# Moving the weight conversion's intermediate word to PSUM, and the products with v beside the scores

## The chip, the cores and the metric

The kernel runs on one core of a Trainium2 chip. The core has a matrix engine (TensorE, PE), a vector engine (VectorE, DVE), a scalar engine (ScalarE, ACT), GpSimd (POOL), and SyncE (SP), whose queue here issues most of the DMAs. Each engine takes its instructions in order and they wait for one another through semaphores. PSUM, into which PE writes, has eight banks of 512 fp32 words for each of 128 partitions. The metric is the device time of the whole program in microseconds, as the median of several executions.

## What is computed

Attention of 4 sequences, 8 heads, 576 positions and 64 dimensions, half the heads with a band of 32 and half with a stride of 32 as mask; then a dense layer pair (512 to 2048 to 512) on the 2304 tokens, and a mixture of 8 experts with two chosen per token. Cut to what matters:

```python
def reference(q, k, v, w_in, w_out, w_gate, w_noise, noise, w1, w2):
    scores = q @ k.transpose(0, 1, 3, 2) / 8              # masked: band of 32, or stride of 32
    attn = softmax(where(mask, scores, -1e9))
    x = merge_heads(attn @ v)                             # 2304 x 512
    h = x @ w_in                                          # 512 -> 2048
    x = (h * sigmoid(1.702 * h)) @ w_out                  # 2048 -> 512
    top2, weight = route(x @ w_gate + softplus(x @ w_noise) * noise)
    for e in range(8):
        for k in range(2):
            m = top2[:, k] == e
            out[m] += weight[m, k] * (relu(x[m] @ w1[e]) @ w2[e])
    return out
```

## The kernel before

The tokens lie in six chunks of 384. The first dense layer pair has 16 pieces `fc` of 128 hidden units; for each chunk and piece `m1_l1` makes the hidden units (12 matmuls of 128x384: three for each of four parts of the model dimension, since every operand is split into a high and a low part) and `m1_l2` adds their share to the output (9 matmuls of 128x512) one iteration later. The order is written out by hand for PE, ACT, DVE and POOL in this part. Chunk 0 is done in two halves (`SEGS`): pieces 0 to 7 (`HALFC` is 8), which I call the first half chunk, then chunk 1, then the rest of chunk 0.

Attention is worked in groups. For one group `scores` makes q·k on PE (L208 or L223), DVE masks them out of PSUM and finds the row's extreme (L171), ACT takes exponents (L176), DVE sums up and inverts (L180, L182), POOL normalizes the early groups (L184), PE transposes the weights (L236 or L241), ACT copies them (L237 or L242), PE multiplies with v (`values`, `g_av`, L254 or L264), and `put_x` splits these products into a high part (ACT, L192) and a low part (DVE, L195). A loop ahead of the first chunk works the first groups; the next ones are threaded into the first half chunk, two in each iteration: behind `m1_l1` PE does products, transposes and scores of three different groups, and behind `m1_l2` the same again.

Weights of the first layer pair arrive as 64-bit words and are converted. A piece is 128x512; `w_bits` does three DVE operations on it: L387 makes an intermediate word `cv` from the high halves, L390 works on it in place, L394 joins it with the low halves into the raw tile `area`. Then ACT casts the result (L361) and POOL forms the low part (L362). The operations of one piece are spread over an iteration (`conv`, one `next` at a time), one piece in odd iterations and two in even ones of the first half chunk; six pieces are converted in the loop ahead of it.

PSUM in the first half chunk: banks 0 and 1 hold the first layer's sums (`ps`), 2 to 4 the second layer's, 5 the scores, 6 the transposes, 7 the products. The loop ahead of it uses 0 to 2 for scores, 3 and 4 for transposes, 5 and 6 for products. `cv` lies in SBUF, in one buffer.

Of the kernel before, what the change touches and what calls it, by code (L numbers as in the profile page):

```python
# [12 lines left out]
I32 = mybir.dt.int32  # L13
# [20 lines left out]
GQ = RPG * NI  # L34
NG = -(-BAND // RPG)
KW = 96
# [63 lines left out]
def tile_kernel(ctx, tc, qkL, qkS, vL, vS, wm1, wm2, wgn, noise, cst, lst0, out):  # L100
# [5 lines left out]
    PB = [psum.tile([128, 512], F32, tag=f"pb{i}", name=f"pb{i}") for i in range(8)]  # L106
# [13 lines left out]
    with ExitStack() as main, tc.manual_schedule(engines={mybir.EngineType.PE}):  # L120
# [4 lines left out]
        tmp = main.enter_context(tc.tile_pool(name="tmp", bufs=2))  # L125
# [8 lines left out]
        def xtile(c):  # L134
            X[c] = xtp.tile([128, 2, 4, CH], F32R, tag="xt", name=f"xt{c}")
# [54 lines left out]
        def put_x(parts, conv):  # L190
            for hi, lo, src in parts:
                nc.scalar.copy(hi, src)  # L192
            next(conv, None)
            for hi, lo, src in parts:
                nc.vector.tensor_sub(lo, src, hi.bitcast(F32))  # L195
# [46 lines left out]
            nc.scalar.copy(pt[:n, :2 * n], PB[bank][:n, :2 * n])  # L242
            return pt

        def g_av(gr, ld, pt, bank, conv):
            b, pr, g = gr
            v = ld[1]
            if pr < 2:
                pb = PB[bank][:, :3 * KW].rearrange("p (t w) -> p t w", w=KW)
                for t in range(3):  # L250
                    for h in range(2):
                        o = 128 * t + 64 * h
                        w = 64
                        nc.tensor.matmul(pb[64 * h:64 * h + 64, t, :w], v[:KW, t, 64 * h:64 * h + 64],  # L254
                                         pt[:KW, o:o + 64], start=True, stop=True)
                c, o = divmod(b * S + 192 * g, CH)
                hi, lo = (X[c][:, i, pr, o:o + 192].rearrange("p (t q) -> p t q", q=64) for i in range(2))
                put_x([(hi, lo, pb[:, :, :64])], conv)
                return
            n = min(GQ, S - GQ * g)  # L260
            nr = n // NI
            pb = PB[bank]
            for h in range(2):
                nc.tensor.matmul(pb[64 * h:64 * h + 64, :n], v[:n, 0, 64 * h:64 * h + 64],  # L264
                                 pt[:n, n * h:n * h + n], start=True, stop=True)
            src = pb[:, :n].rearrange("p (r i) -> p r i", i=NI)
            i0 = 0
            parts = []
            while i0 < NI:
                c, o = divmod(b * S + BAND * i0, CH)  # L270
                ni = min(NI - i0, (CH - o) // BAND)
                hi, lo = (X[c][:, i, pr, o:o + BAND * ni].rearrange("p (i r) -> p r i", r=BAND)
                          [:, RPG * g:RPG * g + nr, :] for i in range(2))
                parts.append((hi, lo, src[:, :, i0:i0 + ni]))
                i0 += ni
            put_x(parts, conv)

        class Attention:
# [34 lines left out]
                    self.pt[i] = g_trans(self.gs[i], self.ld[i], self.sm.pop(i)[0], banks[i % len(banks)])  # L313
                    self.nc += 1

            def values(self, banks, conv=iter(())):
                while self.done < self.nc:
                    i = self.done
                    g_av(self.gs[i], self.ld[i], self.pt.pop(i), banks[i % len(banks)], conv)
                    self.done += 1  # L320


# [48 lines left out]
        def w_step():  # L371
            left = 512
            while PIECES and left:
                fc, s, raw, o, n = PIECES[0]
                if n < 512:
                    if len(done) < born[0] + LATE:
                        return
                    born.pop(0)
                PIECES.pop(0)
                left -= n  # L380
                yield from w_bits(fc, s, raw, o, n)

        def w_bits(fc, s, raw, o, n):
            t = tmp.tile([128, n], I32, tag="cv", name="cv", bufs=1)
            low, high = raw[:, :, 0], raw[:, :, 1]
            w32 = raw.rearrange("p n t -> p (n t)")[:, :n]
            nc.vector.tensor_scalar(t, high, 3, 0x3FFFFFFF,  # L387
                                    op0=OP.logical_shift_left, op1=OP.bitwise_and)
            yield
            nc.vector.scalar_tensor_tensor(t, high, -0x40000000, t,  # L390
                                           op0=OP.bitwise_and, op1=OP.bitwise_or)
            yield

            nc.vector.scalar_tensor_tensor(w32, low, 29, t,  # L394
                                           op0=OP.logical_shift_right, op1=OP.bitwise_or)
            SPLIT[-1].append((fc, s, w32.bitcast(F32), o, n))
            yield
# [10 lines left out]
        def m1_part():  # L408
            for j in range(TPC):
                p = stp.tile([128, DM], F32, tag="raw", name="part")  # L410
                if j == 1:
                    nc.vector.tensor_scalar(p, PB[2 + j], 0.5, None, op0=OP.mult)
                else:
                    nc.scalar.mul(p, PB[2 + j], 0.5)
                PART.append(p)
# [21 lines left out]
        def m1_split(c, t, g):  # L437
            nc.scalar.copy(g[:, 0], t)  # L438
            eng = nc.vector if c or fc >= HALFC else nc.gpsimd
            eng.tensor_sub(g[:, 1], t, g[:, 0].bitcast(F32))  # L440
# [283 lines left out]
        att = Attention(sum(parts, []), upto[1], upto[1])  # L724
# [9 lines left out]
        while att.done < upto[0] - REM:  # L734
            conv = w_step() if k in CONVAT else iter(())
# [37 lines left out]
        def drain():  # L773
            while fill:
                step()

        def finish(c, bank=[7]):
            while att.done < upto[c]:
                att.values([7])
                att.norms()  # L780
                att.transposes([6])

        seq = [(c, fc) for c, a, b in SEGS for fc in range(a, b)]
        for i, (c, fc) in enumerate(seq):
            if i and (c, fc) in FIRST:
                drain()
            if fc == 0:
                for k in {2: (3, 4), 3: (5,)}.get(c, ()):
                    xtile(k)
                if 0 < c < len(parts):  # L790
                    finish(c)
                if c + 1 < len(parts):
                    att.limit = upto[c + 1]
            conv = w_step()
            t, g = m1_l1(c, fc, step, conv)
            att.values([7])
            att.transposes([6])
            next(conv, None)
            att.scores([5])
            next(conv, None)  # L800
            m1_split(c, t, g)
            att.exps()
            for _ in conv:
                pass
            w_split()
            conv = w_step() if i < HALFC and not i % 2 or i >= SMALLS else iter(())
            att.norms(conv)
            if c == 3 and fc in (4, 6, 8, 10, 12):
                clear(x2d, 64 * fc - 256, 1)
            if c == 1 and fc == 12:  # L810
                chained(lst.rearrange("(p n) t -> p (n t)", p=128),
                        lst0.rearrange("(p n) t -> p (n t)", p=128), True)
            if c == 4 and fc % 2:
                clear(out, CH * (fc // 2), min(TPC, NT + NBLK - TPC * (fc // 2)))
            if c == NCHUNK - 1 and fc == 6:
                drain()
                e_list(0, 0, NA // 128, nc.gpsimd)
                fill.append(e_part(0, 0, N + DUMP - CH, wait=WAIT0))
            if c == NCHUNK - 1 and fc == 10:
                e_list(1, 0, NA // 128, nc.gpsimd)  # L820
                pre1 = e_part(1, 0, N + DUMP - CH)
                next(pre1)
            if c == NCHUNK - 1 and fc >= 8:
                w2_load(fc - 8)
            if i:
                m1_l2(*seq[i - 1], step)
                if i == HALFC:
                    m1_part()
                elif seq[i - 1] in LAST:
                    fill.insert(0, routing(seq[i - 1][0], [6], 7))  # L830
            att.values([7], conv)
            next(conv, None)
            att.transposes([6])
            if i < HALFC:
                att.scores([5])
            att.load(2)
            for _ in conv:
                pass
            w_split()
            if i < HALFC:  # L840
                att.exps()
                att.norms()
            if (c, fc) == (NCHUNK - 2, NFC - 1):
                fine.close()
# [38 lines left out]
        for h in range(H0, H1):  # L883
            e, fc = divmod(h, NF2)
# [44 lines left out]
    with tc.tile_pool(name="ovf", bufs=1) as op:  # L929
        n = nc.values_load(nrow[:, 0:1], min_val=0, max_val=NJ)  # L930
        with tc.For_i(0, n, 1) as j:
# [10 lines left out]
            pb = PB[7].rearrange("p (k t) -> p k t", t=128)  # L942
# [3 lines left out]
            w = op.tile([128, NF2, 1024], F32, name="ow")  # L946
# [80 lines left out]
```

## Time and profile before

| | us |
|---|---|
| median of 3 runs | 1027.28 (1025.06 to 1028.02) |
| profiled execution | 1031.41 |
| its span, first to last instruction | 1029.6 |
| PE busy | 994.2 (97%) |
| DVE busy | 489.3 (48%) |
| ACT busy | 394.6 (38%) |
| POOL busy | 219.4 (21%) |

The profile is of one execution, and its span is what the rows below add up to. A busy share over the whole span is a mean over stages with different limits: PE's 97% comes from the long part with the dense layers and the experts, while at the start other engines are the busier ones. The stages that matter here are the loop ahead of the first chunk (to 40.9 us), the first half chunk with early attention in it (to about 94 us, the last of that attention's scores at 81 us), and the rest.

### The profile page before, as it was taken

To read this page: it belongs to the slowest core of one execution; us is meant where nothing else is said; L and a number is where in the kernel's file an instruction comes from. 1 tells how busy PE (TensorE), PEld (TensorE's weight loads), DVE (VectorE), ACT (ScalarE), POOL (GpSimd) and SP (SyncE) were. 2 spreads that over 40 slices of the span, in tenths; PEclk is the share of its full clock that TensorE was granted. 3 is DMA by queue.
4 is the path that set the end of the run, shared out by engine and by line. 5 is a ranking of instruction groups with operands and counts; after the bars stand their busy time and mean duration, and the time that the engine had idled before them with its cause. 6 is when DMAs were issued, how large, how long until landed. Compare 5 with 4: busy or idle time off the path is not lost. (4 is left out here: it accounts for less than half of the span.)

```text
span 1029.6 us, 16148 instructions
## 1 busy us (share of the span) xinstructions
PE 994.2 (97%) x5804; PEld 881.0 (86%) x5804; DVE 489.3 (48%) x1520; ACT 394.6 (38%) x1075; POOL 219.4 (21%) x206
## 2 busy tenths in 40 slices
PE   6999999999999999999999999999999999999996
PEld 5778898988888888899978888989999899998995
DVE  6979864447446544523645353342434343333310
ACT  5665533244444444323433242232424233332311
POOL 3465221102000200200410413040322205041302
PEclk9699999999999999999999999999999999999999
DMA  8835512022131325301342154263544527163403
GB/s 293 281 120 189 175 62 72 1 79 51 47 101 49 70 83 197 109 1 63 78 147 73 32 164 114 81 137 110 122 125 89 157 70 177 62 145 119 84 2 52
DMA packets 63393, 107.69 MB, mean 105 GB/s; under 512 B 12096, under 2 KB 25536, under 8 KB 63296
## 3 DMA queue, kind: packets, MB, share of 16 engines
q1 hardware_dynamic: 53104, 85.63, 26.1%
q0 software_dynamic: 10208, 21.02, 10.7%
q8 instruction: 46, 0.75, 0.3%
q14 instruction: 35, 0.29, 0.1%
HBM read 84.04 MB, written 22.73 MB: 104 GB/s over the span
## 5 line engine op out<-in xcount | busy, mean ns | idle before, releaser
L672 DVE SCALAR_TENSOR_TENSOR ht<-pb,ht 128x384 fp32r<-128x384 f32 (+1 forms) x128 | 62.5, 488 | 251.7 <-ACT ht L671 250.7
L671 ACT ACTIVATE ht<-pb 128x384 fp32r<-128x384 f32 (+1 forms) x128 | 56.0, 437 | 259.4 <-PE pb L670 251.0
L426 PE MATMUL pb<-xt,w 128*128 128x384 f32 x384 | 134.5, 350 | 0.0
L428 PE MATMUL pb<-xt,w 128*128 128x384 f32 x384 | 129.3, 337 | 0.0
L427 PE MATMUL pb<-xt,w 128*128 128x384 f32 x384 | 129.2, 336 | 0.1
L702 POOL DMA_INDIRECT out<-y,ix x40 | 64.9, 1623 | 295.0 <-ACT y L701 262.1
L685 PE MATMUL pb<-w,ht 128*128 128x512 f32 x320 | 127.7, 399 | 0.0
L686 PE MATMUL pb<-w,ht 128*128 128x512 f32 x320 | 125.3, 392 | 0.0
L687 PE MATMUL pb<-w,ht 128*128 128x512 f32 x320 | 125.1, 391 | 0.0
L450 PE MATMUL pb<-w,g 128*128 128x512 f32 x288 | 118.8, 412 | 3.5 <-ACT g L438 2.5
L451 PE MATMUL pb<-w,g 128*128 128x512 f32 x288 | 114.0, 396 | 0.8 <-POOL w L362 0.8
L433 DVE SCALAR_TENSOR_TENSOR th<-th,pb 128x384 f32<-128x384 f32 x96 | 52.9, 551 | 129.9 <-ACT th L431 124.0
L452 PE MATMUL pb<-w,g 128*128 128x512 f32 x288 | 114.6, 398 | 0.0
L575 POOL DMA_INDIRECT lst<-pay,si x36 | 36.3, 1007 | 348.0 <-DVE si L572 292.4
L593 DVE TENSOR_TENSOR w<-raw,w 128x512 fp32r<-128x512 f32 x128 | 84.0, 689 | 18.6 <-ACT w L592 15.3
L431 ACT ACTIVATE th<-pb 128x384 f32<-128x384 f32 x96 | 46.9, 489 | 109.8 <-PE pb L428 101.3
L668 PE MATMUL pb<-xa,w 128*128 128x384 f32 x256 | 87.2, 340 | 0.0
L670 PE MATMUL pb<-xa,w 128*128 128x384 f32 x256 | 86.3, 337 | 0.0
L669 PE MATMUL pb<-xa,w 128*128 128x384 f32 x256 | 85.9, 336 | 0.0
L592 ACT CAST w<-raw 128x512 fp32r<-128x512 f32 x128 | 74.0, 618 | 18.6 <-DMA raw<-wm 14.5
L438 ACT CAST g<-th 128x384 fp32r<-128x384 f32 x96 | 49.3, 513 | 76.7 <-DVE th L433 75.3
L427 PEld LDWEIGHTS pb<-xt,w 128*128 128x128 f32 x384 | 72.5, 189 | 2.6 <-DVE st L180 0.4
(175 smaller groups left out, 1970.9 us busy)
## 6 DMA issues: line engine op xcount, KB each, us to landing
raw<-wm SPq DMA_DIRECT2D x136, 256.0 KB
area<-wm SPq DMA_DIRECT2D x28, 512.0 KB
out<-zero SPq DMA_DIRECT2D x7, 768.0 KB
qk<-qkL SPq DMA_DIRECT2D x16, 304.0 KB
att<-qkS SPq DMA_DIRECT2D x20, 189.0 KB
qk<-qkS SPq DMA_DIRECT2D x20, 189.0 KB
v<-vL SPq DMA_DIRECT2D x16, 192.0 KB
att<-qkL SPq DMA_DIRECT2D x8, 304.0 KB
```

What stands on the lines that cost most here:

```text
L426: nc.tensor.matmul(ps, w[0][:, a], X[c][:, 0, kc, :], start=(kc == 0), stop=False)
L427: nc.tensor.matmul(ps, w[0][:, a], X[c][:, 1, kc, :], start=False, stop=False)
L428: nc.tensor.matmul(ps, w[1][:, a], X[c][:, 0, kc, :], start=False, stop=(kc == 3))
L450: nc.tensor.matmul(o, g[:, 0, a], w[0], start=((c, fc) in FIRST), stop=False)
L451: nc.tensor.matmul(o, g[:, 0, a], w[1], start=False, stop=False)
L452: m = nc.tensor.matmul(o, g[:, 1, a], w[0], start=False, stop=((c, fc) in LAST))
L668: nc.tensor.matmul(ps, w[:, 0, a], x[:, 0, kc, :], start=(kc == 0), stop=False)
L669: nc.tensor.matmul(ps, w[:, 0, a], x[:, 1, kc, :], start=False, stop=False)
L670: nc.tensor.matmul(ps, w[:, 1, a], x[:, 0, kc, :], start=False, stop=(kc == 3))
L685: nc.tensor.matmul(o, g[:, 0, a], w[:, 0, 512:], start=(fc == 0), stop=False)
L686: nc.tensor.matmul(o, g[:, 0, a], w[:, 1, 512:], start=False, stop=False)
L687: m = nc.tensor.matmul(o, g[:, 1, a], w[:, 0, 512:], start=False, stop=(fc == NF2 - 1))
```

## The change

`w_bits` gets its intermediate word from its caller. While the list `INPS` is not empty it is a part of PSUM bank 7, seen as 32-bit integers, and no longer the SBUF tile `cv`; `INPS` is emptied in iteration 8, when the first half chunk's sums have been put away. Since bank 7 then holds that word, the products of `values` go to bank 5, to columns 288 and up, behind the scores, which take columns 0 to 287. In `g_av` the three blocks of a banded group stand 64 columns apart and no longer 96, so that they fit. `finish`, which does single groups at the end of a part, and the loop ahead of the first chunk keep their banks.

```diff
-        def g_av(gr, ld, pt, bank, conv):
+        def g_av(gr, ld, pt, bank, conv, off):
...
-                pb = PB[bank][:, :3 * KW].rearrange("p (t w) -> p t w", w=KW)
+                pb = PB[bank][:, off:off + 192].rearrange("p (t w) -> p t w", w=64)
...
-                put_x([(hi, lo, pb[:, :, :64])], conv)
+                put_x([(hi, lo, pb)], conv)
...
-            pb = PB[bank]
+            pb = PB[bank][:, off:off + GQ]
...
-            def values(self, banks, conv=iter(())):
+            def values(self, banks, conv=iter(()), off=0):
...
-                    g_av(self.gs[i], self.ld[i], self.pt.pop(i), banks[i % len(banks)], conv)
+                    g_av(self.gs[i], self.ld[i], self.pt.pop(i), banks[i % len(banks)], conv, off)
...
+                yield from w_bits(fc, s, raw, o, n, PB[7][:, 512 - left:][:, :n].bitcast(I32) if INPS else None)
                 left -= n
-                yield from w_bits(fc, s, raw, o, n)
-
-        def w_bits(fc, s, raw, o, n):
-            t = tmp.tile([128, n], I32, tag="cv", name="cv", bufs=1)
+
+        INPS = [True]
+
+        def w_bits(fc, s, raw, o, n, t):
+            if t is None:
+                t = tmp.tile([128, n], I32, tag="cv", name="cv", bufs=1)
...
-            att.values([7])
+            vb = [5] if INPS else [7]
+            vo = 3 * KW if INPS else 0
+            att.values(vb, off=vo)
...
                     m1_part()
+                    INPS.clear()
...
-            att.values([7], conv)
+            att.values(vb, conv, vo)
```

No instruction changes its place on any engine. What the instructions write and wait for does. On PE, in iteration 0 behind the first layer, before (`pb_68` is bank 5, `pb_69` bank 6, `pb_70` bank 7; L254 products, L236 transposes, L208 scores; in brackets the semaphores, named by the engine or DMA queue that raises them):

```order
L254 MATMUL pb_70<-att 64x64 [waits DMAHW3_49,DVE_49,Activation_49]
L254 MATMUL pb_70<-att 64x64 x5
L236 MATMUL pb_69<-cs,att 96x128 [waits Pool_49]
L236 MATMUL pb_69<-cs,att 96x128 x2
L208 MATMUL pb_68<-att 128x96 [waits DMAHW1_49]
L208 MATMUL pb_68<-att 128x96 x2
L254 MATMUL pb_70<-att 64x64 [waits DMAHW5_49,DVE_49,Activation_49]
```

On PE at the same place, now:

```order
L254 MATMUL pb_68<-att 64x64 [waits DMAHW3_49,Activation_49]
L254 MATMUL pb_68<-att 64x64 x5
L236 MATMUL pb_69<-cs,att 96x128 [waits Pool_49]
L236 MATMUL pb_69<-cs,att 96x128 x2
L208 MATMUL pb_68<-att 128x96 [waits DMAHW1_49,DVE_49]
L208 MATMUL pb_68<-att 128x96 x2
L254 MATMUL pb_68<-att 64x64 [waits DMAHW5_49,DVE_49,Activation_49]
```

The products have moved to the scores' bank, and the wait for DVE has moved from the products to the scores behind them. In the built program the count that these scores wait for is the one that DVE reaches with L195 of the products two rows above. From the second pair on both have a wait for DVE, before and now; there the scores' count was that of the last masks (L171) and is now that of L195 of the products just made, and the products' count was that of the last L195 and is now that of the last masks.

On DVE, in iteration 0, where two pieces are converted, from the end of the first piece to the reading of the second products, before (`area` is a raw tile, `st` the statistics of a group, `xt` the split products):

```order
L394 SCALAR_TENSOR_TENSOR area<-area,cv 128x512 [waits DVE_49]
L387 TENSOR_SCALAR cv<-area 128x512 [waits DMAHW0_49,DVE_49]
L180 TENSOR_SCALAR st<-st 128x3 [waits Activation_49]
L390 SCALAR_TENSOR_TENSOR cv<-area,cv 128x512 [waits DVE_49]
L182 RECIPROCAL st<-st 128x3 [waits DVE_49]
L394 SCALAR_TENSOR_TENSOR area<-area,cv 128x512 [waits DVE_49]
L195 TENSOR_TENSOR xt_107<-pb_70,xt_107 128x192 [waits Activation_49]
```

On DVE at the same place, now:

```order
L397 SCALAR_TENSOR_TENSOR area<-area,pb_70 128x512 [waits DVE_49]
L390 TENSOR_SCALAR pb_70<-area 128x512 [waits DMAHW0_49,DVE_49]
L180 TENSOR_SCALAR st<-st 128x3 [waits Activation_49]
L393 SCALAR_TENSOR_TENSOR pb_70<-area,pb_70 128x512 [waits DVE_49]
L182 RECIPROCAL st<-st 128x3 [waits DVE_49]
L397 SCALAR_TENSOR_TENSOR area<-area,pb_70 128x512 [waits DVE_49]
L195 TENSOR_TENSOR xt_107<-pb_68,xt_107 128x192 [waits Activation_49]
```

The word is in bank 7 and the order is the same: L195, for which the next scores now wait, stands behind the operations on two pieces. (Lines behind L379 have moved by three or more: L387, L390 and L394 are L390, L393 and L397 in the changed kernel. This text uses the numbers of before.)

## Rows read from the trace of the kernel before

**Rows 1.** Stages: length; busy PE, PEld, DVE, ACT, POOL; PEclk, DMA share, GB/s.

```profile
25.00:40.90 15.90, 13.98 (x73) 10.70 (x73) 15.55 (x71) 11.18 (x52) 7.76 (x11) 0.50 0.98 343
40.90:80.90 40.00, 36.91 (x260) 29.56 (x259) 32.03 (x123) 25.20 (x99) 24.06 (x26) 0.99 0.48 153
80.90:94.00 13.10, 12.80 (x74) 10.34 (x73) 12.05 (x30) 7.07 (x26) 8.63 (x8) 1.00 0.43 152
94.00:1029.60 935.60, 914.07 (x5278) 816.46 (x5276) 414.31 (x1225) 336.11 (x839) 171.61 (x150) 1.00 0.34 93
```

**Rows 2.** Timeline, iteration 4: start us, length us, engine, line, operation, tiles.

```profile
73.30 0.35 PE L264 MATMUL pb<-att 72*64 72x72 f32 x4
...
74.35 0.48 PE L450 MATMUL pb<-w,g 128*128 128x512 f32 x1
...
76.58 0.44 PE L264 MATMUL pb<-att 126*64 126x126 f32 x4
...
77.22 0.60 PE L223 MATMUL pb<-att 128*126 128x126 f32 x4
...
79.77 0.43 DVE L195 TENSOR_TENSOR xt<-pb,xt 128x42 fp32r<-128x42 f32 x2
```

**Rows 3.** DVE's groups by line and shape, 0 to 40.9 us.

```profile
L390 DVE SCALAR_TENSOR_TENSOR cv<-area,cv 128x512 int32<-128x512 int32 x6 | 7.5, 1250 | 0.0
L394 DVE SCALAR_TENSOR_TENSOR area<-area,cv 128x512 int32<-128x512 int32 x6 | 5.1, 850 | 0.2
L387 DVE TENSOR_SCALAR cv<-area 128x512 int32<-128x512 int32 x6 | 4.3, 715 | 0.0
```

**Rows 4.** Timeline of DVE and POOL: a conversion operation beside GpSimd, and undisturbed ones.

```profile
17.97 1.35 POOL L362 TENSOR_TENSOR w<-area,w 128x512 fp32r<-128x512 f32 x1 [1.08 <-ACT w L361]
...
18.22 1.64 DVE L394 SCALAR_TENSOR_TENSOR area<-area,cv 128x512 int32<-128x512 int32 x1
...
48.48 0.43 DVE L387 TENSOR_SCALAR cv<-area 128x512 int32<-128x512 int32 x1
...
48.94 0.69 DVE L390 SCALAR_TENSOR_TENSOR cv<-area,cv 128x512 int32<-128x512 int32 x1
```

**Rows 5.** DVE operations with PSUM as input: L433 to 100 us, L412 whole span.

```profile
L433 DVE SCALAR_TENSOR_TENSOR th<-th,pb x9: 541/547/555, 45.5 to 97.5; 128x384 f32<-128x384 f32 x9
...
L412 DVE TENSOR_SCALAR part<-pb x1: 687/687/687, 101.8 to 101.8; 128x512 f32<-128x512 f32 x1
```

**Rows 6.** Timeline: the first and the last of the eleven scores, and their L195.

```profile
45.74 0.81 PE L208 MATMUL pb<-att 128*128 128x96 f32 x6
...
45.97 0.35 DVE L195 TENSOR_TENSOR xt<-pb,xt 128x192 fp32r<-128x192 f32 x1
...
80.93 0.42 PE L223 MATMUL pb<-att 128*72 128x72 f32 x4
...
82.48 0.45 DVE L195 TENSOR_TENSOR xt<-pb,xt 128x42 fp32r<-128x42 f32 x2
```

**Rows 7.** Timeline: scores B of iterations 0 to 3, and pair A of iteration 1.

```profile
47.51 0.70 PE L223 MATMUL pb<-att 128*126 128x126 f32 x4
...
50.73 0.57 PE L254 MATMUL pb<-att 96*64 96x64 f32 x12 [0.43 <-issue]
...
51.46 0.62 ACT L361 CAST w<-area 128x512 fp32r<-128x512 f32 x1 [2.51 <-PE pb L254]
...
54.38 0.35 DVE L195 TENSOR_TENSOR xt<-pb,xt 128x192 fp32r<-128x192 f32 x1
...
55.80 0.70 PE L223 MATMUL pb<-att 128*126 128x126 f32 x4
...
63.53 0.48 PE L223 MATMUL pb<-att 128*72 128x72 f32 x4 [0.16 <-DVE st L171]
...
70.60 0.65 PE L223 MATMUL pb<-att 128*126 128x126 f32 x4
```

**Rows 8.** Timeline of PE: the idle time ahead of the half clock.

```profile
25.41 0.69 PE L264 MATMUL pb<-att 126*64 126x126 f32 x4 [1.62 <-DVE xt L195]
```

## Prediction

> **What bounds the kernel now.** I read the busy time of each engine by stage first, then the instructions of single iterations in order of time. The table by stage [rows 1] says that from 94.0 us on TensorE (PE) works 914.07 of 935.60 us at a granted clock of 1.00, that is 2.4 GHz: its queue is full there, and whatever is lost earlier the end inherits. From 25.0 to 40.9 us VectorE (DVE) is busy 15.55 of 15.90 us, while PE, at a clock of 0.50 (1.2 GHz), is busy 13.98: this is the attention in front of the first chunk, and DVE bounds it. From 40.9 to 80.9 us the first half chunk runs, with the rest of the early attention threaded between its matmuls: PE is busy 36.91 of 40.00 and has 3.1 us of slack, no more.
>
> An iteration of that half chunk holds two pairs of products with v and scores: pair A behind the first layer, pair B behind the second; I number them by the iteration, from 0. In iteration 4 PE has no gap [rows 2]: products A at 73.30, scores A just ahead of the second layer at 74.35, products B at 76.58, scores B at 77.22. Scores B of iteration 3 began at 70.60 [rows 7], so a dense iteration takes 6.6 us: 2.7 from scores B to products A, 1.05 to the second layer, 2.2 to products B, 0.65 to scores B.
>
> **What the change removes.** The word of 128x512 that the first conversion operation (L387) writes and the other two (L390, L394) read leaves SBUF, where the raw word lies too. Six pieces are converted in the first 40.9 us, L390 at 1250 ns in the mean, L394 at 850, L387 at 715 [rows 3]. Undisturbed they take 0.69 and (L387) 0.43 us [rows 4]; the rest is time beside GpSimd, as when L394 starts at 18.22 us while L362 runs there (from 17.97, for 1.35 us) and takes 1.64. L433, with one input in PSUM and one in SBUF, is never stretched: 541 to 555 ns in nine runs [rows 5]. The two long operations become of that kind.
>
> What will they cost? No row has DVE writing PSUM. Nearest are a tensor_scalar of 128x512 that reads PSUM, 687 ns [rows 5], and the undisturbed L390, 0.69 us. Below that I see no gain, since no row of such a shape with two inputs or one in PSUM is shorter; above, an operation that reads and writes one bank (L390) might take twice as long, 1.4 us. I take 0.69 for all three and keep 1.4 for the range. Then 18 x 0.69 = 12.4 us stand in place of 7.5 + 5.1 + 4.3 = 16.9 [rows 3]: DVE saves 4.5 us. PE caps it: its 13.98 of 15.90 us at half clock leave 1.9 us behind 25.0, and the two pieces before that save some 2. I take **3 us** gained (1 to 4.5; none if L390 takes 1.4, since 6 x 0.7 = 4.2).
>
> **What it adds.** The products leave bank 7, which the word now fills, for the scores' bank 5. The order of instructions stays the same on every engine; PE's waits change. Scores had to wait for the reading of the scores before them; now they wait until DVE's L195 has read the products that PE made just ahead of them, in the same bank though in other columns. PE takes its queue in order, so behind the waiting scores stands a whole first layer (12 matmuls) or second layer (9), the very work with which PE runs ahead of DVE today. Eleven scores, A0 to A5, come to stand so, and PE starts each before its L195 has ended: A0 at 45.74, with the end at 45.97 + 0.35; A5 at 80.93, with the end at 82.48 + 0.45 [rows 6]. Over the eleven this lead adds up to 25.9 us. That would be the price if each L195 stayed where it is; but DVE is late partly because PE ran ahead. So I go round the loop by hand, from the start of scores B (zero), with the durations of these rows.
>
> - *Pair A, plain.* Products at 2.7; tanh 0.5, L433 0.55, L195 0.45 and about 0.2 for hand-overs: scores A at 4.4 in place of 3.4. The second layer follows, products B come at 7.0.
> - *Pair B, odd iteration* (one piece converted). Masks, L394 and the short operations are done by 7.0, ScalarE copies the products, L195 ends at 7.9: scores B at 8.0.
> - *Pair B, even iteration.* A second piece lies ahead of L195 on DVE: masks to 5.6, then L394, L387, L390 and L394 at 0.69 and two short ones at 0.17, L195: scores B at 9.2. In the trace this L195 ends at 79.77 + 0.43, 3.0 us behind the start of scores B at 77.22 [rows 2].
> - *Iterations 1 and 2.* ScalarE's L361 stands ahead of exponents and tanh and waits for products A (idle 2.51 us until L254 [rows 7]); from products A at 50.73 to the end of L195 at 54.38 + 0.35 it is 4.0 us. With 0.26 more for L387, scores A come 2.55 later than in the plain case: 10.5 us for iteration 1, 11.75 for 2.
> - *Iteration 0* has no second layer: products B must also wait for the masks of scores A, and two pieces stand ahead of their L195. Scores B move from 47.51 to 51.35.
>
> Against the trace's scores B at 47.51, 55.80, 63.53, 70.60 and 77.22 and scores A5 at 80.93 [rows 7, 2, 6]: +3.85 for iteration 0, 10.5 - 8.3 = +2.2 for 1, 11.75 - 7.7 = +4.0 for 2, 8.0 - 7.1 = +0.9 for 3, 9.2 - 6.6 = +2.6 for 4, 4.4 - 3.7 = +0.7 for the first part of 5: **+14.2 us**. From below: a plain A costs 1.0 over the dense iteration, an odd B 0.4, an even B 1.6, so 6 x 1.0 + 2 x 0.4 + 3 x 1.6 = 11.6, less the slack of 3.1: 8.5. From above: L390 at 1.4 lies twice on the way of an even B and once of an odd one, 3 x 1.4 + 2 x 0.7 = 5.6 more: 19.8.
>
> Nothing hides it: PE is busy 12.80 of 13.10 us up to 94.0 and nearly always after [rows 1]. Later pieces keep the old form, and the DMAs keep their order, so I cost both at nothing.
>
> In the built program the scores wait although the columns are disjoint. The Trainium skill speaks against this placing too: PSUM — Partial Sum Buffer, section Summary: rules for kernel authors, has PSUM read in another bank than the one a matmul writes, guarded by bank. By that rule the sum stays +14.2; with a guard by columns it would be 0 and the kernel would gain the 3 us.
>
> **The rivals.** (1) *DVE's time wins.* If scores did not really stand (the waits met early, or guarded by columns), the front's 3 us would be left: 1024.3. For it: DVE bounds the stage up to 40.9 us. Against it: tanh, L433 and L195 alone end 1.7 us behind the products, and the eleven waits would have to cost under 1.4 us in all even with the full 4.5 gained. (2) *PE absorbs it.* At the lower bound of the waits and the upper of the gain, less hand-overs that overlap better than I lay them, +5 - 4.5: 1028, which a measurement of this kernel can't tell from no change (0.3%, 3.1 us). (3) *The clock falls too.* PE stood 1.62 us for an L195 up to 25.41 us [rows 8], and the stage from 25.0 on has a clock of 0.50 [rows 1]. I expect three stalls of more than 2 us (B0, A1, A2). If each brings the half clock for the 2.2 us of layer behind it, 3 x 2.2 = 6.6 us more: 1045. Against it: between the stalls PE is denser here than it was there. By the Trainium skill (TensorE: Matmul & The Clock Gate, Part 1: The HAM clock gate) activity releases the throttle and its absence brings it back; long enough stalls would make 1045 the rule.
>
> **How the numbers follow.** -3.0 + 14.2 = +11.2 us. The profiled execution took 1031.41 us (span 1029.6), 4.1 above the median of the runs; I put the difference on the median: 1027.28 + 11.2 = **1038.5 us**. Chances: forecast (+3.1 to +20) 0.66, clock 0.18, absorbed 0.10, DVE's time 0.06. So faster by over 0.3% 0.06, within 0.3% 0.10, slower 0.84. For 8 in 10 I leave out the faster case, most of the absorbed one and the clock rival's upper part: 1029.5 to 1047, the latter being the upper bound, +19.8 without the front's gain.
>
> **What would show it.** Right: the three operations on the word near 0.69 us and none stretched; PE idle ahead of the eleven scores, 1 to 3.6 us each, until L195; the first layer starting about 3 us before 40.89 us, the way from there to scores A5 14 us longer, and what follows as long as before. Wrong: no idle time ahead of these scores; operations of 1.2 us or more on the word, which would eat the gain in front; a clock of 0.50 between 45 and 80 us, which would add rival 3 to the sum.

## The result, and the profile after

The changed kernel takes 1041.28 us (median of four runs, 1040.17 to 1042.15), the kernel before 1026.90 beside it (1025.06 to 1028.02): 14.4 us more, a ratio of 1.0142 with a 95% interval of 1.0124 to 1.0159. The profiled execution took 1040.70 us (span 1038.9), close to its median, while that of before was 4.1 us above its own; so the two traces differ by 9.3 us, and stretches are compared rather than ends. From L387 on, the line numbers of the changed kernel are 3 higher: the word's operations are L390, L393 and L397, the first layer begins at L429 in place of L426, and the second at L453 in place of L450.

The stages of after, cut where the same work begins and ends (first layer 36.88, scores A5 98.30, second chunk 111.1), with the columns of [rows 1]:

```profile
25.00:36.88 11.88, 10.15 (x62) 7.79 (x59) 11.00 (x63) 9.54 (x47) 6.73 (x9) 0.64 1.03 374
36.88:98.30 61.42, 46.39 (x261) 35.85 (x259) 34.05 (x124) 27.35 (x103) 22.78 (x26) 0.82 0.39 126
98.30:111.10 12.80, 12.80 (x72) 10.43 (x73) 9.42 (x25) 6.25 (x21) 6.54 (x7) 1.00 0.32 102
111.10:1038.90 927.80, 911.40 (x5278) 815.84 (x5276) 409.66 (x1224) 335.85 (x838) 171.46 (x150) 1.00 0.35 93
```

The first layer starts 4.0 us earlier than at 40.89 us. From there to scores A5 it takes 61.42 us where before took 40.04 (80.93 - 40.89), at a granted clock of 0.82 in place of 0.99, with PE busy 46.39. That is 4.0 won and 21.4 lost. The second chunk starts at 110.96 us against 93.90: 17.1 late in these two traces. In the medians 14.4 us are left at the end.

DVE's groups on the word in the front (0 to 36.9 us), against [rows 3]:

```profile
L393 DVE SCALAR_TENSOR_TENSOR pb<-area,pb 128x512 int32<-128x512 int32 x6 | 4.1, 688 | 0.0
L390 DVE TENSOR_SCALAR pb<-area 128x512 int32<-128x512 int32 x6 | 4.1, 687 | 0.0
L397 DVE SCALAR_TENSOR_TENSOR area<-area,pb 128x512 int32<-128x512 int32 x6 | 4.1, 687 | 0.2
```

The sum is 12.3 us in place of 16.9. No operation is stretched any more; L393, which reads and writes one bank, is at 688 ns not longer than the others.

PE's timeline: the first layer's start, and the eleven scores with the idle time ahead of each:

```profile
36.88 0.67 PE L429 MATMUL pb<-xt,w 128*128 128x384 f32 x1
...
42.50 0.91 PE L208 MATMUL pb<-att 128*128 128x96 f32 x6 [0.47 <-DVE xt L195]
...
47.26 1.22 PE L223 MATMUL pb<-att 128*126 128x126 f32 x4 [1.97 <-DVE xt L195]
...
56.54 1.21 PE L223 MATMUL pb<-att 128*126 128x126 f32 x4 [3.25 <-DVE xt L195]
...
63.25 0.70 PE L223 MATMUL pb<-att 128*126 128x126 f32 x4 [0.41 <-DVE xt L195]
...
70.23 1.22 PE L223 MATMUL pb<-att 128*126 128x126 f32 x4 [3.43 <-DVE xt L195]
...
76.87 0.48 PE L223 MATMUL pb<-att 128*72 128x72 f32 x4 [0.47 <-DVE xt L195]
...
81.09 0.70 PE L223 MATMUL pb<-att 128*126 128x126 f32 x4 [0.84 <-DVE xt L195]
...
85.20 0.70 PE L223 MATMUL pb<-att 128*126 128x126 f32 x4 [0.71 <-DVE xt L195]
...
89.50 0.70 PE L223 MATMUL pb<-att 128*126 128x126 f32 x4 [0.84 <-DVE xt L195]
...
93.92 0.70 PE L223 MATMUL pb<-att 128*126 128x126 f32 x4 [0.93 <-DVE xt L195]
...
98.30 0.48 PE L223 MATMUL pb<-att 128*72 128x72 f32 x4 [0.84 <-DVE xt L195]
```

Every one stands for L195 (PE sits idle, with these scores next in its queue), as the prediction said; in the trace of before none of the eleven did. Eight stand under 1 us, three (B0, A1, A2) 2 to 3.4. Why A1 stands that long is seen in all engines between its products and its start:

```profile
52.26 0.57 PE L254 MATMUL pb<-att 96*64 96x64 f32 x12
...
52.99 0.62 ACT L361 CAST w<-area 128x512 fp32r<-128x512 f32 x1 [7.18 <-PE pb L254]
...
54.29 0.47 ACT L434 ACTIVATE th<-pb 128x384 f32<-128x384 f32 x1
...
55.09 0.67 DVE L390 TENSOR_SCALAR pb<-area 128x512 int32<-128x512 int32 x1
...
55.67 0.54 DVE L436 SCALAR_TENSOR_TENSOR th<-th,pb 128x384 f32<-128x384 f32 x1
...
56.13 0.35 DVE L195 TENSOR_TENSOR xt<-pb,xt 128x192 fp32r<-128x192 f32 x1
```

ScalarE's cast waits for products A, and then its queue is worked off in order (cast, exponents, tanh); DVE's L436 waits for tanh, and L195 stands behind both. From products to scores it is 4.3 us, in which PE has a product and a transpose to do.

The granted clock (the column after POOL) in stretches around the three long stands:

```profile
45.00:53.00 8.00, 6.03 (x33) 5.28 (x32) 2.71 (x10) 0.77 (x4) 0.67 (x1) 0.57 0.15 45
53.00:56.00 3.00, 0.29 (x3) 0.04 (x1) 1.55 (x4) 2.33 (x8) 1.87 (x2) 0.94 0.03 7
56.00:63.00 7.00, 6.30 (x27) 4.62 (x27) 2.69 (x11) 2.33 (x8) 2.84 (x3) 0.54 0.33 104
63.00:69.50 6.50, 3.55 (x22) 2.90 (x22) 2.13 (x9) 2.50 (x10) 1.83 (x2) 0.99 0.27 91
69.50:76.50 7.00, 6.17 (x19) 4.26 (x19) 4.62 (x15) 1.85 (x8) 1.64 (x3) 0.53 0.20 75
76.50:98.30 21.80, 17.25 (x105) 13.35 (x105) 13.88 (x56) 12.33 (x46) 9.91 (x11) 1.00 0.43 142
```

Behind each long stand the scores and the whole next layer run at half clock (1.2 GHz): the second layer behind A1 takes from 57.41 to the products at 61.53, 4.1 us, where the one behind A3, at 2.4 GHz, takes 2.25 (81.55 to 83.80).

### The profile page after: what moved, and what is told of

It is laid out like the page before. It is cut to its first block, busy times and chain, and to the rows that moved or that the text cites. A ratio compares the mean times of both kernels' runs of the same rounds, so it can differ in the third digit from the quotient of the medians.

```text
span 1038.9 us, 16150 instructions
## 1 busy us (share of the span) xinstructions
PE 997.3 (96%) x5804; PEld 883.7 (85%) x5804; DVE 480.1 (46%) x1520; ACT 395.9 (38%) x1075; POOL 216.4 (21%) x206
## 3 DMA queue, kind: packets, MB, share of 16 engines
HBM read 84.04 MB, written 22.73 MB: 103 GB/s over the span
## 5 line engine op out<-in xcount | busy, mean ns | idle before, releaser
L429 PE MATMUL pb<-xt,w 128*128 128x384 f32 x384 | 135.7, 353 | 0.0
L453 PE MATMUL pb<-w,g 128*128 128x512 f32 x288 | 119.8, 416 | 1.5 <-ACT w L361 0.8
L436 DVE SCALAR_TENSOR_TENSOR th<-th,pb 128x384 f32<-128x384 f32 x96 | 53.0, 552 | 133.9 <-ACT th L434 133.6
L596 DVE TENSOR_TENSOR w<-raw,w 128x512 fp32r<-128x512 f32 x128 | 83.8, 689 | 16.2 <-ACT w L595 16.1
L429 PEld LDWEIGHTS pb<-xt,w 128*128 128x128 f32 x384 | 73.2, 191 | 2.5
```

The costliest lines, as they stand in the source:

```text
L429: nc.tensor.matmul(ps, w[0][:, a], X[c][:, 0, kc, :], start=(kc == 0), stop=False)
L453: nc.tensor.matmul(o, g[:, 0, a], w[0], start=((c, fc) in FIRST), stop=False)
```

## Experiments

All kernels below start from the changed one; diffs are against it. Each was timed beside the kernel before, whose median was 1029.14 us for the first four, 1027.87 for the next four and 1028.54 for the last two. "Loop" is the time from the first layer's start to scores A5 in the profiled execution (before: 40.04 us), the clock is that of the loop. A loop is read from a single trace, and its first part alone, up to scores B0, takes 6.4 to 7.5 us in the traces that share no bank there. The expectations reckon from 1026.90 us for the kernel before; what is compared is each kernel's difference from the kernel before beside it.

| kernel | median, us | against before, 95% interval | loop, us | clock |
|---|---|---|---|---|
| word ahead only | 1025.17 | 0.9946 to 0.9982 | 40.46 | 1.00 |
| shared bank only | 1045.27 | 1.0129 to 1.0194 | 58.67 | 0.87 |
| shared from iteration 3 | 1029.01 | 0.9990 to 1.0030 | 46.42 | 0.97 |
| filler in the stalls | 1039.03 | 1.0066 to 1.0127 | 53.93 | 1.00 |
| changed kernel again | 1042.74 | 1.0140 to 1.0188 | 61.42 | 0.82 |
| products beside layer 1 | 1022.58 | 0.9939 to 0.9970 | 40.71 | 0.95 |
| next layer in the bank | 1031.34 | 1.0021 to 1.0055 | 46.26 | 0.93 |
| one stall | 1025.06 | 0.9964 to 0.9991 | 44.33 | 0.88 |
| one stall, filled | 1025.85 | 0.9950 to 0.9981 | 41.93 | 0.96 |
| one stall, again | 1027.08 (one run) | | 42.38 | 0.95 |

**The gain alone.**

```diff
             w_split()
             k += 1
+        INPS.clear()
```

> The word of the conversion lies in PSUM bank 7 only in the loop ahead of the first chunk, where nothing else uses that bank; from the first layer on it is back in SBUF and the products have bank 7 for themselves. My theory (the word is a gain, the shared bank the whole loss): the first layer starts near 36.9 us as in the changed kernel (before: 40.89), no scores stand for L195, the clock stays at 1.00 in the first half chunk, and the time is 1026.9 - 4.0 = 1022.9 us (1021.5 to 1024.5). Rival (what the front gains is lost again, since PE then waits for transfers or weights): 1027. Rival (the word in PSUM itself holds DVE or PE up): 1030 or more.

Measured: 4.0 us under the kernel before, as expected. The first layer starts at 36.55 us, the loop has no stand for L195, and the word's operations in front (DVE's groups, 0 to 36.55 us; then PE's timeline) take what they take in the changed kernel:

```profile
L397 DVE SCALAR_TENSOR_TENSOR area<-area,pb 128x512 int32<-128x512 int32 x6 | 4.1, 687 | 0.2
L393 DVE SCALAR_TENSOR_TENSOR pb<-area,pb 128x512 int32<-128x512 int32 x6 | 4.1, 686 | 0.0
```

```profile
36.55 0.43 PE L429 MATMUL pb<-xt,w 128*128 128x384 f32 x1
```

So the word in PSUM is a gain where the bank is free anyway, and the gain reaches the end.

**The loss alone.**

```diff
-                yield from w_bits(fc, s, raw, o, n, PB[7][:, 512 - left:][:, :n].bitcast(I32) if INPS else None)
+                yield from w_bits(fc, s, raw, o, n, None)
```

> The word stays in SBUF throughout; only the products move into the scores' bank for the first half chunk. My theory: the waits and the clock are as in the changed kernel and the front's gain of 4.0 us is missing, so 1041.3 + 4.0 = 1045.3 us (1043 to 1048, up if a conversion operation ahead of L195 is stretched by GpSimd); the scores stand for L195 with idle times of 2 to 3.5 us at B0, A1 and A2 and a clock of 0.50 behind them. Rival (the word in PSUM, not the shared bank, delays the products' readers): 1027, no such idle times.

Measured: 16.1 us over the kernel before beside it, where the changed kernel is 14.9 over it in the other group of runs. The waits need no word in PSUM (PE's timeline, scores B0, A1 and A2; B0 was expected at 2 us or more):

```profile
50.79 1.22 PE L223 MATMUL pb<-att 128*126 128x126 f32 x4 [1.71 <-DVE xt L195]
60.03 1.21 PE L223 MATMUL pb<-att 128*126 128x126 f32 x4 [3.00 <-DVE xt L195]
...
72.28 0.70 PE L223 MATMUL pb<-att 128*126 128x126 f32 x4 [3.17 <-DVE xt L195]
```

But I had expected the word to be worth 4 us in the difference, and the medians have 1 to 2. Their intervals are too wide to rule 4 out; the traces bear the small value out, with scores A5 at 99.15 us here and at 98.30 and 98.95 us in the two traces of the changed kernel, although the changed kernel's front is 3 to 3.6 us shorter. The three long stands are 0.25 us shorter each than in the changed kernel, because the first operation takes 412 ns in SBUF in the loop, and 680 in PSUM (DVE's group of the loop):

```profile
L390 DVE TENSOR_SCALAR cv<-area 128x512 int32<-128x512 int32 x9 | 3.7, 412 | 0.1
```

The loop is 2.75 us shorter in all (58.67 against 61.42). Some 0.75 of that are these stands; the rest goes with a clock that comes back earlier (0.87 against 0.82), and as the kernel with one stall below shows that this differs between executions of one kernel, it isn't shown to be the word's doing. In this loop the word in PSUM is a loss, since there the two long operations are hardly stretched in SBUF (686 and 730 ns in the mean) and the first one comes just ahead of L195. By the Trainium skill (VectorE: DVE Perf Modes, Why PSUM operands drop a tier) any operand in PSUM keeps DVE out of the mode that uses both SBUF read ports; the two means agree with that, while the reason is shown by no run.

**The plain iterations alone.**

```diff
+        INPS.clear()
...
-            vb = [5] if INPS else [7]
-            vo = 3 * KW if INPS else 0
+            share = 3 <= i <= HALFC
+            vb = [5] if share else [7]
+            vo = 3 * KW if share else 0
...
-                    INPS.clear()
```

> Like the kernel with the word in PSUM ahead of the first chunk only, but from iteration 3 of the first half chunk on the products share the scores' bank (word in SBUF there). My theory: the plain iterations cost what they cost in the changed kernel, 1.3 us for iteration 3, 2.1 for 4 and 0.7 for the first part of 5, 4.0 us together, by waits of 0.7 to 0.9 us each, and the clock stays at 1.00: 1022.9 + 4.0 = 1026.9 us (1025.5 to 1028.5). Rival (every shared pair brings the half clock as soon as it is the first to stand): 4.0 + 2 to 4 us more, 1029 to 1031, with a clock of 0.50 somewhere between iterations 3 and 5. Rival (waits under a microsecond are taken up by PE's slack of 3.1 us): 1023 to 1024.

Measured: 3.8 us over the kernel with the word ahead only, and a clock of 1.00 from iteration 3 on. The first shared pair pays more than it did in the changed kernel, 1.56 us of idle time instead of 0.84, as DVE is further behind PE when no pair has been held back before (PE's timeline, scores A3 and B3):

```profile
65.74 0.70 PE L223 MATMUL pb<-att 128*126 128x126 f32 x4 [1.56 <-DVE xt L195]
69.85 0.70 PE L223 MATMUL pb<-att 128*126 128x126 f32 x4 [0.72 <-DVE xt L195]
```

Its loop is 6.0 us longer than that of the kernel with the word ahead only, some 2 us more than the medians differ by; the last point of the account below comes back to this.

**The clock alone.**

```diff
+        def filler(n):
+            for _ in range(n):
+                nc.tensor.matmul(PB[(i + 1) % 2][:, :CH], X[0][:, 0, 0, :128], X[0][:, 0, 0, :],
+                                 start=True, stop=True)
...
+            filler({1: 18, 2: 19}.get(i, 0))
             att.scores([5])
...
+                filler({0: 11}.get(i, 0))
                 att.scores([5])
```

> The changed kernel with matmuls that nothing reads (11, 18 and 19 of 128x384, 0.17 us apart at the full clock) ahead of scores B of iteration 0 and scores A of iterations 1 and 2, where PE stood 1.97, 3.25 and 3.43 us. They end a little before those waits do. Clock theory (my third rival): PE stays at 1.00, the three layers behind the waits take 2.3 us in place of 4.1 and the scores 0.4 less each, and some 6.5 us come back: 1041.3 - 6.5 = 1034.8 us (1033.5 to 1037). Rival (PE's speed there does not matter, since the chain through ScalarE and DVE sets the pace): 1041, with the clock at 1.00 all the same. Rival (the clock falls whatever PE does): clock 0.50 as before and 1041 to 1043.

Measured: 9.9 us over the kernel before, 4.5 to 5 less than the changed kernel, where I had expected 6.5. The waits are still there, filled; the clock is 1.00 over the loop (the loop's row by engine; then PE's timeline at scores A1, L788 being the filler):

```profile
36.36:90.29 53.93, 46.46 (x308) 37.34 (x308) 33.88 (x127) 27.75 (x104) 22.84 (x26) 1.00 0.47 150
```

```profile
49.83 3.39 PE L788 MATMUL pb<-xt 128*128 128x384 f32 x18
53.35 0.70 PE L223 MATMUL pb<-att 128*126 128x126 f32 x4
```

Within the loop the two differ by 61.42 - 53.93 = 7.5 us. Of these, 7.1 lie behind scores B0 (98.30 - 47.26 = 51.04 us against 90.29 - 46.32 = 43.97) and are the clock's price behind the three stands; 0.4 lie ahead of B0, where the first layer began at half clock in the trace of after and at full clock here. 13.9 us (53.93 - 40.04) are the waits', and the medians say the same: 1039.03 - 1025.17 = 13.9 us over the kernel with the word ahead only. That PE's speed does not matter there is refuted.

**The changed kernel on the chip of the others.** The file is unchanged.

> The changed kernel once more, beside the others on one chip. If the difference is the kernel's and not a chip's, it stands 14.4 us over the kernel before here too (12.5 to 16). With the shared bank alone 16.1 us over the kernel before, the word in PSUM is worth 1.7 us net, less than the 4 us of the front, since in the loop its first operation takes 0.67 us in place of 0.41.

Measured: 14.9 us over the kernel before, with the same loop to a hundredth (61.42 us). The difference is the kernel's, not a chip's.

**Another bank to share.**

```diff
+        INPS.clear()
...
+            if i == 2:
+                INPS.append(True)
...
-            vb = [5] if INPS else [7]
-            vo = 3 * KW if INPS else 0
-            att.values(vb, off=vo)
+            va = [(i + 1) % 2] if INPS else [7]
+            vb = [i % 2] if INPS else [7]
+            vo = CH if INPS else 0
+            att.values(va, off=vo)
```

> The word in PSUM ahead of the first chunk, in SBUF for iterations 0 and 1, and again in PSUM bank 7 from iteration 2 to the end of the half chunk; there the products share a bank too, but the spare columns of a first layer's bank whose next matmuls come at least one layer later (pair A: the bank of the next first layer, pair B: that of the one after). My theory (what costs is not that a bank is shared, but that PE's next instruction writes to it): no scores and no layer stand for L195, clock 1.00, and the time is that of the word in PSUM ahead of the first chunk only, 4.0 us under the kernel before, within 1.5 us either way. Rival (a shared bank costs as such, through DVE's reading while PE is to write): 4 us more than that, with idle times ahead of products or layers.

(The banded groups of iterations 0 and 1 need 192 columns and don't fit into the 128 that a layer of 384 leaves in its bank.)

Measured: 5.3 us under the kernel before, faster than both kernels of this study. Products share a bank in both pairs of iterations 2 to 8, and nothing stands for L195 (PE's timeline, products and scores A2):

```profile
56.73 0.44 PE L264 MATMUL pb<-att 126*64 126x126 f32 x4
...
57.40 0.60 PE L223 MATMUL pb<-att 128*126 128x126 f32 x4
```

Its loop takes 40.71 us, 0.7 longer than that of before: its first layer, which started only at 38.15 us, ran at a clock of 0.50, and the expected 1.00 holds from 46 us on. Whether it beats the kernel with the word ahead only isn't told apart: the two intervals overlap.

**The same, with one bank exchanged.**

```diff
             va = [(i + 1) % 2] if INPS else [7]
-            vb = [i % 2] if INPS else [7]
+            vb = [(i + 1) % 2] if INPS else [7]
```

(this diff is against the kernel just shown)

> As the kernel with the products beside the first layer, with one thing changed: from iteration 2 on the products of pair B go to the bank into which the very next first layer writes. My theory: that layer now stands until L195 has read the products, from the trace of before up to 2.9, 1.45 and 2.6 us in iterations 2, 3 and 4 (end of L195 less the layer's start), less once DVE has caught up, and so on to the half chunk's end: 4 to 9 us over the other kernel, the idle times now ahead of the first layer's first matmul. Rival (the layer is not held, or the time is taken up later): the same time as the other kernel within 1.5 us.

Measured: 8.8 us over it. Now the first layer stands, ahead of its first matmul, behind pair B of iterations 2 and 4 (PE's timeline):

```profile
63.64 0.44 PE L429 MATMUL pb<-xt,w 128*128 128x384 f32 x1 [2.65 <-DVE xt L195]
...
80.14 0.45 PE L429 MATMUL pb<-xt,w 128*128 128x384 f32 x1 [1.32 <-DVE xt L195]
```

Later ones follow at 86.96 and 93.94 us, 0.60 and 1.58 long. The same products in the same columns cost nothing in the bank that PE writes a layer later, and 8.8 us in the bank that it writes next. Part of the 8.8 is the clock, which is at 0.50 from 65 to 67 us and again from 95 to 98.

**One stall, three ways.** First the products share the scores' bank in pair A of iteration 2 alone:

```diff
+        INPS.clear()
...
-            vb = [5] if INPS else [7]
-            vo = 3 * KW if INPS else 0
+            vb = [7]
+            vo = 0
+            if i == 2:
+                att.values([5], off=3 * KW)
```

> The word in PSUM ahead of the first chunk only, and the products share the scores' bank just once, in pair A of iteration 2. My theory (one long stand is enough for the clock): scores A2 stand some 3 us, the clock is 0.50 for the second layer behind them, 4.1 us in place of 2.2; 3.5 us of wait and 2 of clock, less about 1 us that PE's later gaps take up, so 4.5 us (3 to 6) over the kernel without any sharing. Rival (one stand does not bring the clock down, it took several): clock 1.00 and 2 to 3 us. Rival (a single stand is taken up by the slack): under 1 us.

Then the same file again, for another trace:

> The kernel with one stall once more, for its trace. Theory (the clock falls behind one stand of 3 us in some executions only): the clock may be 1.00 behind scores A2 this time, with the step of iteration 2 at 10 to 10.5 us in place of 12.5. Rival (it falls each time): 0.50 again, and 12.5 us.

And with the stall filled (`filler` as above):

```diff
+            filler({2: 17}.get(i, 0))
             att.scores([5])
```

> As the kernel with one stall, with 17 matmuls of 128x384 that nothing reads ahead of scores A2, where PE stood 3.12 us; they end a little before the wait does. That kernel's trace had the clock at 0.50 for the layer behind the stall and its execution took 1028.3 us, while eight of its ten executions took 1023.9 to 1025.8. Theory (in most of its executions the clock did not fall, and one stall is worth 1 to 2 us without the clock): here the clock stays at 1.00, the step of iteration 2 is 2 to 2.5 us shorter than the 12.5 us of that trace, and the median is 2.0 to 3.5 us under the kernel before, as for the kernel with one stall (2.8 under). Rival (the clock fell in all of them): another 2 us come off, 4.5 to 5.5 us under the kernel before.

Scores A2 and B2 in PE's timeline, of the kernel with one stall, of the same again, and of the filled one:

```profile
60.06 1.22 PE L223 MATMUL pb<-att 128*126 128x126 f32 x4 [3.12 <-DVE xt L195]
...
65.87 0.42 PE L223 MATMUL pb<-att 128*72 128x72 f32 x4
```

```profile
59.26 1.22 PE L223 MATMUL pb<-att 128*126 128x126 f32 x4 [3.14 <-DVE xt L195]
64.19 0.42 PE L223 MATMUL pb<-att 128*72 128x72 f32 x4
```

```profile
60.02 0.70 PE L223 MATMUL pb<-att 128*126 128x126 f32 x4 [0.17 <-DVE xt L195]
63.37 0.42 PE L223 MATMUL pb<-att 128*72 128x72 f32 x4
```

Scores A2 stand 3.12 and 3.14 us, and the half clock follows both times. From A2 to B2 it is 5.81, 4.93 and 3.35 us, so the half clock behind one long stand costs 1.6 to 2.5 us of that step. In the medians none of this shows: 2.8 us under the kernel before with the stall, 2.7 with the stall filled, each uncertain by about 1.5 us. The kernel with one stall is 1.2 us over the one without any sharing, each against the kernel before beside it, where I had expected 4.5 (3 to 6), although its loop is 3.9 and 1.9 us longer in its two traces. The step of iteration 2, from scores B1 to B2, takes 12.50, 11.65 and 10.09 us in the three traces; the second lies between what my theory (10 to 10.5) and its rival (12.5) had said of it. That the clock falls in some executions only is borne out by neither trace of that kernel, but both are of executions above its median (1028.34 and 1027.08 us against 1025.06), and two don't refute it; the 2 us that the rival to it had coming off with the filled stall did not come off either. It stays open where they go.

## Why the prediction was right, and where not

The time, 1041.28 us, lies 2.8 above the forecast of 1038.5 and within the range, and the sign and the mechanism are as forecast: scores stand for L195, and that costs far more than the front gains. One step failed, the clock, which I had left out of the sum, and it is partly luck that the time came out so near all the same. In the traces, -4.0 (front) + 13.9 (waits) + 7.5 (clock in the loop) make +17.4 us at scores A5, 3.0 more than the +14.4 of the medians. From medians alone the terms are -4.0 (word ahead only) + 13.9 (stalls filled, over that) + 5.0 (changed kernel, over stalls filled) = +14.9, the last two uncertain by some 4 us each.

- **The price of the operations** (0.69 us each): 684 to 689 ns in the mean of the nineteen pieces that went through PSUM (687 and 688 in front). That L393 might take twice as long in one bank was an empty bound.
- **The front's gain** (-3.0, 1 to 4.5): -4.0. The two parts that I named, 1.9 and some 2, came out, and the 3 that I took for their sum was too low. The products that PE starts at 25.41 us in before [rows 8] start at 22.73 now, 2.7 us earlier, and from there to the first layer it is 14.15 us (36.88 - 22.73) in place of 15.48, another 1.3:

```profile
22.73 0.44 PE L264 MATMUL pb<-att 126*64 126x126 f32 x4 [0.53 <-DVE xt L195]
```

  The start isn't fixed to a tenth: with the same front it is 36.36 to 38.15 us in ten traces here.
- **The waits** (+14.2): 13.9 without the fall of the clock. By steps, predicted and measured with the stalls filled: iteration 0 6.62 + 3.85 = 10.5 and 9.96, iteration 1 10.5 and 11.12, iteration 2 11.75 and 11.42, iteration 3 8.0 and 8.35, iteration 4 9.2 and 8.70, the part of 5 4.4 and 4.38. Going round the loop by hand held to 0.6 us in each step; the sum of the leads, 25.9, would have been nearly twice too much. What I said of the idle times (1 to 3.6 us at each of the eleven) was wrong for eight of them, 0.41 to 0.93; my own sum had the plain pairs cost only 0.4 to 1.6.
- **The clock** (rival 3, put at 0.18 and left out of the sum): it fell behind just the three stands that the rival named, for 7.1 us where it had 6.6. The step that failed is the argument against it, that PE is denser between the stalls: PE did work on, and the clock fell all the same. The row of before that bore on it was [rows 8], a single stand of 1.62 us with half clock behind it, and I had three longer ones in the sum. A second one in the trace of before answers the argument itself and stands neither in the rows nor in the prediction: in the middle of the dense layers, behind 3.6 us without a gap at a clock of 1.00, PE stood 2.55 us, and over the next 3.8 us the clock was 0.55 (PE's timeline, then the stretches ahead of and behind the stand):

```profile
526.19 0.54 PE L450 MATMUL pb<-w,g 128*128 128x512 f32 x1 [2.55 <-ACT g L438]
```

```profile
520.00:523.60 3.60, 3.60 (x19) 3.06 (x17) 1.85 (x3) 1.44 (x3) 0.31 (x1) 1.00 0.95 316
526.20:530.00 3.80, 3.80 (x9) 2.73 (x10) 2.95 (x6) 1.88 (x4) 0.00 (x0) 0.55 0.49 160
```

  The Trainium skill (TensorE: Matmul & The Clock Gate, Part 1: The HAM clock gate) has it that activity releases the throttle and its absence brings it back; the trace agrees, with a clock of 0.53 to 0.57 around the three stands and 1.00 where they are filled.
- **Nothing behind the loop** (0): the changed kernel is 17.1 us late at the second chunk in the traces, and 14.4 at the end in the medians. The two don't compare well, since the trace of before is late for its kernel at its end: no other trace has a stand like that of 2.55 us just shown (the longest behind 112 us in any of them is 1.4). From scores A5 to the end it is 948.7 us in before, 940.6 and 941.6 in the two traces of the changed kernel and 942.3 to 947.9 in the nine others, and the 942.3 are of products beside layer 1, which had nothing to give back. PE's 914.07 busy of 935.60 us in [rows 1] leave 21.5 us of idle time behind 94 us, and I treated that as if nothing in it could shrink. In the trace of after, PE's two waits for ScalarE's copy (L264 behind L242, 1.9 us in before) are missing, and of four waits for a gather (1.9 us) one of 0.5 is left:

```profile
PE pb L635 <- DMA g<-x2d,ix: 1.9, 4, 0.6
PE pb L264 <- ACT pt L242: 1.9, 2, 1.0
```

```profile
PE pb L638 <- DMA g<-x2d,ix: 0.5, 1, 0.5
```

  (PE's waits behind the first half chunk, of before and of after: us in total, times, the longest.) The wait for the copy is missing in one trace of the kernel with one stall and there in the other, so it differs between executions of one kernel. That a late start makes such waits fewer is not shown, nor that what the loop lost comes back by it; the filled kernel gave nothing back. This part stays open.

Of the rivals, "DVE's time wins" did not happen here, but it is what the kernel with the word ahead only shows: 4.0 us gained, where that rival had 3. "PE absorbs it" fell by the waits' size alone.

## What to carry to other kernels

When a tile moves into a bank, ask which instruction of PE writes to that bank next and who must have read it by then: here a bank whose next writer comes a layer later was shared for nothing, and the one that PE writes next held up its whole queue. (The wait is one that the built program puts in, also for columns that don't overlap; whether the chip needs it there is tested by no run.) Price a stand of TensorE with the layer behind it at half clock as long as no row shows that the clock survives such a stand. And take a scratch tile out of SBUF only for the stretch in which DVE sets the end and beside GpSimd is stretched; in the loop the first operation took 0.68 us for it in place of 0.41.

## What was not expected of the hardware

- The half clock of the front comes and goes by execution: with the same work up to the first layer, the stage from 25.0 us on has a granted clock of 0.92 in one trace (word ahead only) and 0.63 in another (products beside layer 1), and the first layer starts 1.6 us apart.
- Behind one stand of 3.12 us the clock was at 0.50 up to 65 us, behind one of 3.14 us in another execution of the same kernel it was back at 1.00 from 63 us on. The length of a stand alone doesn't order what follows: behind 1.32 us (next layer in the bank, at 80.14 us) and 1.56 us (shared from iteration 3) the clock was 1.00, behind 1.43 us (word ahead only, in front, at 20.25 us), 1.58 us (next layer in the bank, at 93.94 us), 1.62 us [rows 8] and 1.71 us (shared bank only) it was 0.50.
- A DVE operation that reads and writes the same bank (L393) takes 683 to 695 ns, 689 in the mean; one that only reads it (L397) takes 684 in the mean.
